# Memory attention and a gated convolution in one kernel: a new written order of all steps

## The chip, the cores and the metric

The kernel runs on one core of a Trainium2 chip. The core has TensorE (PE, with its weight loads PEld), VectorE (DVE), ScalarE (ACT), GpSimd (POOL) and SyncE (SP, which here only issues the DMAs). The metric is the device time in microseconds of one execution; less is better.

## What is computed

For each of 8 batches: attention over 32 memory slots per head (8 heads of 64 columns, 576 rows), then a gated convolution on the 512 joined columns.

```
a    = softmax(phi, axis=rows)                 # 576 x 32 per head
k_m, v_m = a.T @ k, a.T @ v                    # 32 x 64 per head
p    = softmax(q @ k_m.T / 8)                  # 576 x 32 per head
x    = p @ v_m, heads side by side             # 576 x 512
gate = sigmoid(sum over 5 taps of conv_w[k] * x shifted by k)
out  = (gate * (x @ w_val)) @ w_out
```

All inputs and the output are float32. conv_w, w_val and w_out are shared by all batches.

## The kernel before, in words

The body is a list of small functions, called steps (`@step`), and a string `ORDER` with 950 names. The last loop of the kernel walks through `ORDER` and calls each step with the numbers behind its name; `phi_max.0.1` is `phi_max(0, 1)`: batch 0, half 1. A star behind a name (`soft_sub.0.0*`) makes `pick(usual, other)` return the second engine that the step knows. Each engine works through its own instructions in the order in which the steps issued them, and waits by semaphores for what others make; so `ORDER` alone decides what stands in front of what on PE, DVE, ACT, POOL and in SP's one DMA queue. The order had been made by a planner outside the kernel; the planner is not part of it.

The steps of one batch b, in the order of the data (g is a half of the heads, s a half of the 576 rows, t and n a block of 128 columns, y a pair of blocks):

- `load_phi`, `load_kv`, `load_rest`, `load_q` issue DMAs. `phi_max` (DVE, L343) takes maxima, `phi_turn` (PE, L354) turns them, `phi_top` (DVE, L361) finishes, `phi_spread` (PE, L370) spreads them to all partitions, `phi_lay` (ACT) copies them, `phi_sub` (POOL, with a star DVE, L383) and `phi_exp` (ACT, L388) make the weights. For batch 0 these steps run by halves g.
- `slots` (PE, L397) multiplies the weights with k, v and a column of ones; `slots_inv` (DVE, L404 and L406) inverts the sums, `slots_scale` (DVE, or ACT with a star) scales, `slots_turn` (PE) and `slots_place` (ACT) turn the result into kvT.
- `scores` (PE, L447) multiplies q with it; `scores_turn` (DVE, L459) transposes 32x32 blocks into the tile st. Then the softmax over 32 slots: `soft_max` (DVE, L485), `soft_sub` (POOL, L492, DVE with a star), `soft_exp` (ACT, L497), `soft_sum` (DVE, L503), `soft_inv` (a small addition, L512 on DVE or L510 on ACT with a star, and the inverse L513), `soft_mul` (POOL, DVE with a star, L519), `soft_turn` (DVE, L525), which writes pT. For batch 0 they run by halves of the rows, so that `soft_turn.0.0` and `soft_turn.0.1` each give half of pT. `soft_high` (ACT) and `soft_low` (POOL, DVE with a star, L217) split pT into a rounded part pH and the rest pL.
- `val_rows` (PE, L547) multiplies v_m with w_val; `val_copy`, `val_high`, `val_low` bring it out of PSUM and split it (vwF, vwH, vwL).
- `value` (PE, L642, six matmuls) makes a block of x @ w_val. The gate of batch 0 is `taps` (products, L572), `conv` (PE, L585, 40 matmuls a half) and `sigmoid` (ACT, L632); those of the others are `mix` (PE, L598), five `tap` steps (ACT, then DVE L622; a star gives the last tap to ACT and POOL) and `open_gate` (ACT).
- `gated` (DVE L655, with a star ACT and POOL) multiplies value and gate, `gated_high` and `gated_low` split it (hH, hL), `project` (PE, L675, twelve matmuls) multiplies with w_out, `place` (ACT, with a star DVE) copies to SBUF, `store` issues the DMA out.

The shared weights come as float32 and are rounded in steps of their own: `load_w` (w is c, v or o for conv_w, w_val, w_out; block t), `narrow_size` (ACT, L273) and `narrow_round` (ACT, L286), `narrow_bits` (DVE, L278), `narrow_add` (POOL, L292), `narrow_done` (DVE, L301). conv_w then goes through `spread_taps` (PE, L308) and `place_taps` (ACT), w_out through `wo_high` (ACT) and `wo_low` (POOL, L217). `warm.n` (PE, L224) issues n matmuls whose result nobody reads.

PSUM holds four tiles b (one bank each) and two tiles cv (two banks each); conv and mix take both cv tiles, scores takes them as well, and a step that needs one waits until the last reader of it is done. Of raw weights four fit in SBUF, of k and v three halves.

```
    def pick(usual, other):
        return other if live["other"] else usual

    with tc.manual_schedule():
        for x in ORDER.split():
            name, *args = x.rstrip("*").split(".")
            live["other"] = x.endswith("*")
            steps[name](*(int(a) if a.isdigit() else a for a in args))
```

The functions as the program prints them:

Of the kernel before, what the change touches and what calls it, by code (L numbers as in the profile page):

```python
# [43 lines left out]
warm.8 phi_exp.0.0 narrow_round.v.2 place_taps.0 narrow_bits.v.2 narrow_add.v.2 narrow_done.v.2 slots.0.0
slots_inv.0.0 slots_scale.0.0* narrow_done.v.3 slots.0.1 slots_inv.0.1 load_w.v.1 narrow_size.v.1 spread_taps.1
load_q.0.0 narrow_round.v.1 place_taps.1 load_q.0.1 warm.2 slots_scale.0.1 slots_turn.0 slots_place.0 load_w.o.0
narrow_bits.v.1 narrow_add.v.1 scores.0 narrow_done.v.1 narrow_round.o.0 taps.0.0 scores_turn.0.0 load_w.o.2
narrow_size.o.0 soft_max.0.0 soft_sub.0.0* taps.0.1 narrow_bits.o.0 narrow_size.o.2 narrow_bits.o.2 turn_taps.0
lay_taps.0 load_kv.1.1 soft_exp.0.0 scores_turn.0.1 narrow_round.o.2 narrow_add.o.0 val_rows.0 phi_exp.1 load_rest.1
slots.1.1 soft_sum.0.0 soft_inv.0.0 soft_mul.0.0* val_copy.0.1 soft_turn.0.0 soft_max.0.1 soft_sub.0.1* val_copy.0.0  # L50
val_high.0.0 val_low.0.0* load_w.o.1 narrow_size.o.1 narrow_bits.o.1 soft_high.0.0 soft_low.0.0* soft_exp.0.1
load_w.o.3 narrow_add.o.2 val_high.0.1 val_low.0.1 narrow_round.o.3 narrow_size.o.3 soft_sum.0.1 soft_inv.0.1*
narrow_bits.o.3 conv.0.0 sigmoid.0.0.1 load_kv.1.0 soft_mul.0.1* soft_turn.0.1 slots.1.0 sigmoid.0.0.0 soft_high.0.1
slots_inv.1.1 slots_scale.1.1* slots_inv.1.0 slots_scale.1.0* narrow_add.o.3 narrow_done.o.3 load_phi.2 conv.0.1
slots_turn.1 phi_max.2 phi_turn.2 soft_low.0.1 value.0.0.1 phi_top.2 narrow_round.o.1 narrow_add.o.1 slots_place.1
sigmoid.0.1.1 sigmoid.0.1.0 phi_spread.2 narrow_done.o.2 phi_lay.2 phi_sub.2 narrow_done.o.1 wo_high.1 wo_low.1
load_q.1 scores.1.0 wo_high.2 gated.0.0.1 scores_turn.1.0 scores.1.1 scores_turn.1.1 val_rows.1 val_copy.1.0
val_copy.1.1 soft_max.1 soft_sub.1 load_phi.3 value.0.1.0 gated.0.1.0 phi_max.3 value.0.0.3 gated.0.0.3 value.0.0.2
gated.0.0.2 value.0.0.0 gated.0.0.0 narrow_done.o.0 value.0.1.1 phi_exp.2 phi_turn.3 phi_top.3 wo_low.2 soft_exp.1
soft_sum.1 val_high.1.0 load_rest.2 value.0.1.3 gated_high.0.0.0 gated_low.0.0.0 load_kv.2.1 slots.2.1 load_kv.2.0  # L60
slots.2.0 slots_inv.2.1 gated.0.1.1 wo_high.3 soft_inv.1* soft_mul.1* soft_turn.1 slots_scale.2.1* gated.0.1.3
gated_high.0.0.1 gated_low.0.0.1 slots_inv.2.0 slots_scale.2.0 phi_spread.3 phi_lay.3 wo_high.0 wo_low.0 wo_low.3
value.0.1.2 warm.2 soft_high.1 load_phi.4 gated.0.1.2 val_low.1.0 phi_max.4 mix.1.1 tap.1.1.1.0* tap.1.1.1.1
tap.1.1.1.2 tap.1.1.1.3 project.0.0.0 slots_turn.2 gated_high.0.1.0 place.0.0.0 gated_high.0.1.1 soft_low.1 load_q.2
gated_low.0.1.0 project.0.0.1 phi_turn.4 slots_place.2 val_rows.2 tap.1.1.0.0 tap.1.1.0.1 load_kv.3.1 tap.1.1.1.4
tap.1.1.0.2 val_high.1.1 val_low.1.1 place.0.0.1 val_copy.2.0 val_high.2.0 scores.2.0 open_gate.1.1.1 scores_turn.2.0
val_low.2.0 val_copy.2.1 project.0.0.3 place.0.0.3 tap.1.1.0.3 tap.1.1.0.4 gated_low.0.1.1 scores.2.1 project.0.0.2
place.0.0.2 scores_turn.2.1 mix.1.0 tap.1.0.0.0 phi_top.4 value.1.1.3 soft_max.2 gated.1.1.3 soft_sub.2 tap.1.0.0.1
tap.1.0.0.2 tap.1.0.1.0* tap.1.0.1.1 project.0.1.0 tap.1.0.1.2 tap.1.0.1.3 phi_sub.3 load_rest.3 tap.1.0.1.4
soft_exp.2 value.1.0.2 store.0.0.1 soft_sum.2 soft_inv.2 soft_mul.2 project.0.1.1 place.0.1.0 place.0.1.1 val_high.2.1  # L70
project.0.1.3 phi_spread.4 tap.1.0.0.3 tap.1.0.0.4 phi_lay.4 phi_exp.3 phi_sub.4 value.1.1.2 place.0.1.3 gated.1.1.2
soft_turn.2 project.0.1.2 open_gate.1.1.0 place.0.1.2 open_gate.1.0.1 slots.3.1 slots_inv.3.1 slots_scale.3.1
load_kv.3.0 slots.3.0 gated_high.1.1.1 slots_inv.3.0 gated_low.1.1.1 slots_scale.3.0 gated.1.0.2 open_gate.1.0.0
# [671 lines left out]
```

## Time and profile before

| what | us |
|---|---|
| median of 3 timed runs | 252.17 |
| lowest and highest of them | 251.85, 253.33 |
| the profiled execution, its own time | 251.45 |
| its span (first to last instruction) | 249.70 |

The profile shows one execution. Its span lies 1.75 us under its own time, which also holds the start and the end of the program. Lines as L343 are lines of the kernel; DVE is VectorE, ACT ScalarE, POOL GpSimd; times of rows are us from the start of the span unless marked ns. A matmul's end is modelled, so a busy PE need not be a PE at its peak; where the number of matmuls in a stretch counts, the start of the next one is used.

### The profile page before, as it was taken

How to read it: one execution, taken by the hardware profiler on the slowest of the kernel's cores; microseconds unless marked ns; L12 is line 12 of the kernel's file. 1: busy time of each engine (PE TensorE's matmuls, PEld its weight loads, DVE VectorE, ACT ScalarE, POOL GpSimd, SP SyncE). 2: the span in 40 equal slices, each digit the busy share in tenths (PEclk: the TensorE clock that was granted, in tenths of full speed). 3: DMA queues.
4: the chain of work that ended last, by engine and by line, in shares of the span. 5: the costliest groups of instructions: out<-in, count | busy, mean ns of one | idle time of the engine just before them, and what ended most of it. 6: DMA issues, size and time to landing. Idle time of an engine off the chain costs nothing.

```text
span 249.7 us, 6632 instructions
## 1 busy us (share of the span) xinstructions
PE 230.2 (92%) x2664; PEld 199.8 (80%) x2664; DVE 205.9 (82%) x413; ACT 182.5 (73%) x350; POOL 171.0 (68%) x128
## 2 busy tenths in 40 slices
...
GB/s 215 418 414 406 410 272 277 217 139 367 15 350 376 398 251 105 257 371 198 31 361 191 50 50 182 131 239 128 112 3 95 3 0 97 174 18 1 142 97 95
DMA packets 12142, 47.78 MB, mean 191 GB/s; under 512 B 1352, under 2 KB 1864, under 8 KB 9168
## 3 DMA queue, kind: packets, MB, share of 16 engines
...
## 4 chain that ended last, share of the span: by engine, by line
PE 73%; DVE 18%; ACT 2%; POOL 2%; issue 2%; DMA 1%; SPq 0%; POOLq 0%; DVEq 0%; ACTq 0%
PE b L675 39%; PE b L642 18%; PE cv L598 4%; PE b L397 3%; PE cv L447 3%; PE b L547 2%; DVE pT L525 2%; DVE st L519 2%; DVE gate L622 2%; DVE mx L343 1%; DVE ss L503 1%; DMA raw<-in_conv_w_dram 1%; PE cv L585 1%; DVE hH L301 1%; DVE st L459 1%
## 5 line engine op out<-in xcount | busy, mean ns | idle before, releaser
L622 DVE SCALAR_TENSOR_TENSOR gate<-cv,cwP,gate 128x288 f32<-128x288 f32 x200 | 87.4, 504 | 3.2 <-ACT gate L620 3.1
L675 PE MATMUL b<-hL,woH 128*128 128x288 f32 x256 | 76.4, 299 | 0.2 <-PE cv L598 0.2
L675 PE MATMUL b<-hH,woL 128*128 128x288 f32 x256 | 76.1, 297 | 0.0
L675 PE MATMUL b<-hH,woH 128*128 128x288 f32 x256 | 75.4, 294 | 0.0
L217 POOL TENSOR_TENSOR hL<-h,hH 128x576 fp32r<-128x576 f32 x31 | 44.8, 1455 | 12.1 <-ACT hH L214 7.0
L675 PEld LDWEIGHTS b<-hL,woH 128*128 128x128 f32 x256 | 48.1, 188 | 5.1 <-issue 2.0
L675 PEld LDWEIGHTS b<-hH,woL 128*128 128x128 f32 x256 | 48.1, 188 | 0.2 <-POOL woL L217 0.2
L675 PEld LDWEIGHTS b<-hH,woH 128*128 128x128 f32 x256 | 48.1, 188 | 0.0
L214 ACT COPY o<-b 128x288 f32<-128x288 f32 x50 | 19.6, 404 | 26.9 <-PE b L675 25.9
L642 PE MATMUL b<-pL,vwH 128*128 128x288 f32 x128 | 29.4, 311 | 0.0
L655 POOL TENSOR_TENSOR h<-h,gate 128x288 f32<-128x288 f32 x20 | 16.0, 809 | 17.6 <-ACT h L653 17.2
L642 PE MATMUL b<-pH,vwL 128*128 128x288 f32 x128 | 27.3, 295 | 0.0
L642 PE MATMUL b<-pH,vwH 128*128 128x288 f32 x128 | 27.3, 294 | 0.0
L655 DVE TENSOR_TENSOR h<-b,gate 128x288 f32<-128x288 f32 x44 | 18.9, 448 | 9.0 <-ACT gate L627 4.3
L620 ACT ACTIVATE gate<-cv,cwP 128x288 f32<-128x288 f32 x56 | 24.8, 506 | 0.4 <-PE cv L598 0.2
L642 PEld LDWEIGHTS b<-pL,vwH 128*128 128x128 f32 x128 | 20.1, 188 | 5.2 <-issue 1.7
L292 POOL TENSOR_TENSOR hH<-hH,hL 128x512 int32<-128x512 int32 (+1 forms) x9 | 12.8, 1424 | 16.4 <-DVE hH L278 9.0
L217 POOL TENSOR_TENSOR vwL<-vwF,vwH 128x512 fp32r<-128x512 f32 x14 | 18.4, 1313 | 8.1 <-ACT vwH L214 4.7
L627 ACT ACTIVATE gate<-gate 128x576 f32<-128x576 f32 x28 | 19.4, 696 | 5.4 <-DVE gate L622 4.5
L397 PE MATMUL b<-kv,e 128*32 128x129 f32 x512 | 19.0, 293 | 2.8 <-ACT e L388 2.7
L397 PEld LDWEIGHTS b<-kv,e 128*32 128x32 f32 x512 | 15.4, 141 | 7.2 <-ACT e L388 4.9
L642 PEld LDWEIGHTS b<-pH,vwL 128*128 128x128 f32 x128 | 20.5, 188 | 0.0
...
## 6 DMA issues: line engine op xcount, KB each, us to landing
...
```

What stands on the lines that cost most here:

```text
L214: eng.copy(out=out, in_=x) if eng is nc.scalar else eng.tensor_copy(out=out, in_=x)
L217: eng.tensor_tensor(out=out, in0=x, in1=hi.bitcast(F32), op=ALU.subtract)
L292: nc.gpsimd.tensor_tensor(out=a, in0=a, in1=r, op=ALU.add)
L397: nc.tensor.matmul(km[j * M:(j + 1) * M, 0:2 * D + 1], lhsT=e[:, g, j * M:(j + 1) * M, c], rhs=x[:, c, j, :] if c < C - 1 else rests[b % 2 ...
L447: nc.tensor.matmul(sc[t][j * M:(j + 1) * M, c, 0:HALF], lhsT=live["kvT", b][rows, x, j * M:(j + 1) * M], rhs=live["q", b][rows, x, j, :], ...
L598: nc.tensor.matmul(cv[g][x * D:(x + 1) * D, j // 2, 0:PAD + HALF], lhsT=live["kvd", b][rows, G, g], rhs=pTs[b % 2][rows, g, s * HALF:(s + ...
L620: nc.scalar.activation(out=o[:, t], in_=x, func=AF.Identity, scale=w)
L622: nc.vector.scalar_tensor_tensor(out=o[:, t], in0=x, scalar=w, in1=o[:, t], op0=ALU.mult, op1=ALU.add)
L627: nc.scalar.activation(out=gt, in_=gt, func=AF.Sigmoid)
L642: nc.tensor.matmul(vp[:, 0:HALF], lhsT=a[:, t // PG, n:n + P], rhs=p[:, g, s * HALF:(s + 1) * HALF], start=(i == 0), stop=(i == len(parts) ...
L655: eng.tensor_tensor(out=h[:, i], in0=x, in1=gt, op=ALU.mult)
L675: nc.tensor.matmul(ps[:, 0:HALF], lhsT=w[:, t, n * P:(n + 1) * P], rhs=a[:, t % 2], start=(i == 0), stop=(i == len(parts) - 1))
```

## The change

Only the string `ORDER` is new; it holds the same 950 steps. No function, tile or buffer count changes, and since the string has one line more, every line of the kernel below it has a number that is higher by 1. 45 steps lose their star and 47 others get one, so some steps change engine: `soft_sub.0.0` and `soft_sub.0.1` go from DVE to POOL, `taps.0.0` and `taps.0.1` from POOL to DVE, `soft_mul.6` from DVE to POOL, `val_copy` of batches 5 to 7 in one half each from ACT to DVE; 9 instead of 12 gates have the starred tap.

```diff
-load_phi.0.0 phi_max.0.0 phi_turn.0.0 load_phi.0.1 load_w.c.0 narrow_size.c.0 narrow_bits.c.0 phi_max.0.1 phi_turn.0.1
...
+load_phi.0.0 phi_max.0.0 phi_turn.0.0 phi_top.0.0 load_w.v.2 narrow_round.v.2 narrow_size.v.2 narrow_bits.v.2
+load_w.c.0 narrow_add.v.2 narrow_round.c.0 load_w.v.0 load_w.v.3 narrow_round.v.3 narrow_done.v.2 phi_spread.0.0
...
```

The DMA queue of SP, at the start of the program. First as it stood before (e is phi, raw a block of weights, kv and rest are k and v with their last rows):

```order
L234 DMA e<-in_phi_dram 128x640 x2
L259 DMA raw<-in_conv_w_dram 8x640
L234 DMA e<-in_phi_dram 128x1280
L259 DMA raw<-in_w_val_dram 128x1024 x3
L239 DMA kv_78<-in_kv_dram 128x2064
L244 DMA rest_81<-in_rest_dram 128x516
L239 DMA kv_79<-in_kv_dram 128x2064
L259 DMA raw<-in_w_val_dram 128x1024
L249 DMA q<-in_q_dram 128x1152 x2
```

and now:

```order
L235 DMA e<-in_phi_dram 128x640
L260 DMA raw<-in_w_val_dram 128x1024
L260 DMA raw<-in_conv_w_dram 8x640
L260 DMA raw<-in_w_val_dram 128x1024 x2
L235 DMA e<-in_phi_dram 128x640
L245 DMA rest_81<-in_rest_dram 128x516
L235 DMA e<-in_phi_dram 128x1280
L240 DMA kv_78<-in_kv_dram 128x2064
L240 DMA kv_79<-in_kv_dram 128x2064
L260 DMA raw<-in_w_val_dram 128x1024
L260 DMA raw<-in_w_out_dram 128x1024
L250 DMA q<-in_q_dram 128x1152 x2
L260 DMA raw<-in_w_out_dram 128x1024
```

Three blocks of w_val now stand behind the first half of phi and ahead of its second half, of all of batch 1's phi and of the first k and v; the fourth stays behind the second kv, and a block of w_out has moved ahead of q.

DVE, from the first transposition of batch 0's scores on (twelve rows each; st are scores, mm their maxima, ss their sums, pT the turned result). Before:

```order
L459 STREAM_TRANSPOSE st<-cv 128x2x288
L485 TENSOR_REDUCE mm<-st 128x18
L492 TENSOR_TENSOR st<-st,mm 128x2x288
L278 TENSOR_SCALAR hH<-hH 128x512 x2
L459 STREAM_TRANSPOSE st<-cv 128x2x288
L503 TENSOR_REDUCE ss<-st 128x18
L512 TENSOR_SCALAR ss<-ss 128x18
L513 RECIPROCAL ss<-ss 128x18
L519 TENSOR_TENSOR st<-st,ss 128x2x288
L525 STREAM_TRANSPOSE pT_74<-st 128x2x288
L485 TENSOR_REDUCE mm<-st 128x18
L492 TENSOR_TENSOR st<-st,mm 128x2x288
```

and now:

```order
L460 STREAM_TRANSPOSE st<-cv 128x2x288
L486 TENSOR_REDUCE mm<-st 128x18
L460 STREAM_TRANSPOSE st<-cv 128x2x288
L486 TENSOR_REDUCE mm<-st 128x18
L302 SCALAR_TENSOR_TENSOR hH<-raw,hH 128x512
L504 TENSOR_REDUCE ss<-st 128x18
L513 TENSOR_SCALAR ss<-ss 128x18
L514 RECIPROCAL ss<-ss 128x18
L279 TENSOR_SCALAR hH<-hH 128x512
L520 TENSOR_TENSOR st<-st,ss 128x2x288
L504 TENSOR_REDUCE ss<-st 128x18
L526 STREAM_TRANSPOSE pT_74<-st 128x2x288
```

Both halves are now transposed and searched for their maxima before either is summed; before, the second half's maximum stood behind the first half's way into pT (L525). The two subtractions L492 are no longer on DVE.

DVE around the softmax of batch 6, near 180 us. Before (o are finished blocks, hH rounded gated values):

```order
L503 TENSOR_REDUCE ss<-st 128x36
L214 COPY o<-b 128x288
L214 CAST hH<-h 128x576
L513 RECIPROCAL ss<-ss 128x36
L519 TENSOR_TENSOR st<-st,ss 128x1152
L525 STREAM_TRANSPOSE pT_74<-st 128x2x576
```

and now:

```order
L504 TENSOR_REDUCE ss<-st 128x36
L513 TENSOR_SCALAR ss<-ss 128x36
L514 RECIPROCAL ss<-ss 128x36
L623 SCALAR_TENSOR_TENSOR gate<-cv,cwP,gate 128x288 x4
L215 COPY o<-b 128x288
L623 SCALAR_TENSOR_TENSOR gate<-cv,cwP,gate 128x288 x2
L526 STREAM_TRANSPOSE pT_74<-st 128x2x576
```

The multiplication of st (L519) has left DVE, for POOL, and seven instructions, six for the taps and one for a block of output, stand between the inverse and the transposition.

## Rows read from the trace of the kernel before

**Rows 1.** The head of the page, the busy time of each engine over the span (with its share and number of instructions), and from the costliest groups VectorE's product of a value block with its gate (busy us and mean ns of one, then idle time before).

```profile
span 249.7 us, 6632 instructions
...
PE 230.2 (92%) x2664; PEld 199.8 (80%) x2664; DVE 205.9 (82%) x413; ACT 182.5 (73%) x350; POOL 171.0 (68%) x128
...
L655 DVE TENSOR_TENSOR h<-b,gate 128x288 f32<-128x288 f32 x44 | 18.9, 448 | 9.0 <-ACT gate L627 4.3
```

**Rows 2.** The busy time by stage. Columns: the stretch from and to in us, its length, then for each engine the busy us and the number of instructions, then the granted clock of TensorE as a share of full, the busy share of the DMA engines and GB/s.

```profile
0.00:24.19 24.19, 14.71 (x165) 10.53 (x165) 14.24 (x25) 11.34 (x21) 9.89 (x19) 1.00 0.93 362
24.19:37.65 13.46, 10.01 (x181) 6.65 (x180) 12.81 (x23) 10.60 (x18) 6.21 (x5) 0.62 0.83 341
37.65:56.14 18.49, 16.50 (x271) 13.28 (x271) 16.89 (x28) 14.16 (x27) 13.65 (x10) 1.00 0.60 212
56.14:178.79 122.65, 122.55 (x1419) 107.16 (x1420) 111.97 (x237) 107.75 (x209) 108.50 (x74) 1.00 0.56 210
178.79:184.18 5.39, 4.71 (x99) 4.29 (x97) 5.31 (x6) 2.39 (x4) 2.25 (x2) 1.00 0.15 58
184.18:246.13 61.95, 61.76 (x535) 57.85 (x535) 44.73 (x98) 35.88 (x72) 30.46 (x22) 1.00 0.18 67
246.13:249.70 3.57, 0.00 (x0) 0.00 (x0) 0.00 (x0) 0.40 (x1) 0.00 (x0) 1.00 0.29 98
```

**Rows 3.** The chain of work that ended last, in order of time: start us, us, what (engine, tile, line).

```profile
54.76 1.39 DVE pT L525
...
56.20 0.75 PE cv L598 x16
...
180.24 2.48 DVE st L519
...
184.18 0.83 PE cv L598 x16
...
246.13 0.40 ACT o L214
```

**Rows 4.** Instructions in order of time, all engines, 0 to 26 us: start us, us, engine, line, operation, out<-in, count, and in brackets the idle time before it and what ended it.

```profile
3.61 0.82 DVE L343 TENSOR_REDUCE mx<-e 128x128 f32<-128x640 f32 x1 [3.61 <-DMA e<-in_phi_dram]
...
4.70 0.48 ACT L273 ACTIVATE hH<-raw 8x320 f32<-8x320 f32 x1 [2.67 <-DMA raw<-in_conv_w_dram]
...
8.32 0.66 ACT L286 ACTIVATE hL<-raw 128x512 int32<-128x512 uint32 x1 [2.76 <-DMA raw<-in_w_val_dram]
...
10.85 1.43 PE L308 MATMUL b<-taps,kvT 8*128 8x320 f32 x2
...
11.16 0.41 DVE L278 TENSOR_SCALAR hH<-hH 128x512 int32<-128x512 int32 x1
...
11.72 1.27 POOL L292 TENSOR_TENSOR hH<-hH,hL 128x512 int32<-128x512 int32 x1 [4.59 <-DVE hH L278]
...
13.02 0.69 DVE L301 SCALAR_TENSOR_TENSOR w_val_sb<-raw,hH 128x512 int32<-128x512 int32 x1 [1.12 <-POOL hH L292]
...
15.65 1.51 DVE L278 TENSOR_SCALAR hH<-hH 128x512 int32<-128x512 int32 x1
...
16.25 1.76 PE L397 MATMUL b<-kv,e 128*32 128x129 f32 x32
...
22.84 2.15 POOL L572 TENSOR_TENSOR taps<-cwB,kvd 128x320 f32<-128x320 f32 x2
...
22.94 1.33 DVE L301 SCALAR_TENSOR_TENSOR w_val_sb<-raw,hH 128x512 int32<-128x512 int32 x1 [1.50 <-POOL hH L292]
...
24.19 0.77 DVE L459 STREAM_TRANSPOSE st<-cv 128x576 f32<-128x576 f32 x1
```

**Rows 5.** The same view from 25 to 38 us, VectorE and, in the second row, ScalarE.

```profile
25.00 0.75 DVE L485 TENSOR_REDUCE mm<-st 128x18 f32<-128x576 f32 x1
...
26.57 0.68 ACT L497 ACTIVATE st<-st 128x576 f32<-128x576 f32 x1 [1.63 <-DVE st L492]
...
27.83 0.70 DVE L503 TENSOR_REDUCE ss<-st 128x18 f32<-128x576 f32 x1
...
28.57 1.07 DVE L512 TENSOR_SCALAR ss<-ss 128x18 f32<-128x18 f32 x1
...
29.98 0.76 DVE L519 TENSOR_TENSOR st<-st,ss 128x576 f32<-128x576 f32 x1
...
30.77 0.78 DVE L525 STREAM_TRANSPOSE pT<-st 128x576 f32<-128x576 f32 x1
...
36.87 0.78 DVE L525 STREAM_TRANSPOSE pT<-st 128x576 f32<-128x576 f32 x1
```

**Rows 6.** The same view for rows of GpSimd, ScalarE and VectorE between 26 and 54 us, and as the last row VectorE's maximum over a whole batch's scores between 56 and 246 us from the groups by line and form (busy us and mean ns of one, idle before).

```profile
26.96 2.65 POOL L292 TENSOR_TENSOR hH<-hH,hL 128x512 int32<-128x512 int32 x2 [1.96 <-DVE hH L278]
...
35.61 1.28 ACT L632 ACT_TABLE_LOAD   x1
...
46.90 2.15 POOL L492 TENSOR_TENSOR st<-st,mm 128x1152 f32<-128x1152 f32 x1
...
49.04 1.80 DVE L301 SCALAR_TENSOR_TENSOR hH<-raw,hH 128x512 int32<-128x512 int32 x1
...
53.37 1.36 DVE L519 TENSOR_TENSOR st<-st,ss 128x1152 f32<-128x1152 f32 x1
...
L485 DVE TENSOR_REDUCE mm<-st 128x36 f32<-128x1152 f32 x6 | 8.1, 1345 | 0.1
```

More of the change, by code (lines that the diff above doesn't have):

```diff
@@ L44 @@
[L44 to L73, printed above, removed]
@@ new lines @@
+tap.1.1.1.4 phi_max.4 soft_high.1 scores.2.0 scores_turn.2.0 place.0.0.1 scores_turn.2.1 project.0.1.0 phi_exp.3
+phi_turn.4 load_kv.3.0 place.0.1.1* phi_top.4 soft_max.2 place.0.1.0 mix.1.0 tap.1.0.0.0* load_kv.3.1 store.0.1.0
+slots.3.0 slots_inv.3.0 tap.1.0.0.1 soft_low.1 slots_scale.3.0* tap.1.0.0.2 val_rows.2 val_copy.2.1 tap.1.0.0.3
+slots.3.1 val_copy.2.0 slots_inv.3.1 soft_sub.2 load_q.3 value.1.1.0 gated.1.1.0 soft_exp.2 soft_sum.2 tap.1.0.1.0
+tap.1.0.1.1 project.0.1.3 slots_scale.3.1* place.0.1.3 value.1.1.1 tap.1.0.0.4 gated.1.1.1* soft_inv.2* tap.1.0.1.2
@@ new lines @@
+phi_spread.4 soft_mul.2 tap.1.0.1.3 project.0.1.2 load_phi.5 phi_max.5 val_high.2.1 project.0.0.3 load_rest.4
+slots_turn.3 open_gate.1.0.0 phi_lay.4 phi_sub.4 place.0.1.2 place.0.0.3 value.1.0.0 store.0.0.1 slots_place.3
+gated_high.1.1.0 tap.1.0.1.4 soft_turn.2 val_high.2.0 open_gate.1.1.1 value.1.1.3 gated_low.1.1.0 gated.1.1.3*
+scores.3.0 scores_turn.3.0 open_gate.1.0.1 gated.1.0.0* scores.3.1 scores_turn.3.1 soft_high.2 value.1.1.2 gated.1.1.2
+value.1.0.2 mix.2.1 gated.1.0.2* value.1.0.1 gated_high.1.1.1 gated_low.1.1.1 load_kv.4.0 tap.2.1.0.0 tap.2.1.1.0
@@ new lines @@
+tap.2.0.0.2 project.1.1.1 tap.2.0.1.0* tap.2.0.1.1 tap.2.0.1.2 tap.2.0.1.3 soft_low.2 load_kv.5.1 val_low.3.1
+project.1.0.1 place.1.0.1 open_gate.2.1.1 tap.2.0.0.3 tap.2.0.0.4 project.1.1.0 slots_scale.4.1* place.1.1.0
+place.1.1.1 project.1.0.0 place.1.0.0 soft_mul.3 soft_turn.3 phi_spread.5 tap.2.0.1.4 open_gate.2.1.0 value.2.1.3
+phi_lay.5 slots_turn.4 slots_place.4 val_high.3.0 value.2.1.1 value.2.1.2 gated.2.1.2 soft_high.3 gated.2.1.1
+value.2.1.0 store.1.1.0 gated.2.1.0 mix.3.1 tap.3.1.0.0 phi_sub.5 gated_high.2.1.0* gated_low.2.1.0 val_low.3.0
@@ new lines @@
+store.3.0.0 slots.7.1 slots_inv.7.1 gated.5.0.1 slots.7.0 gated_low.5.1.0 slots_inv.7.0 soft_high.6* soft_low.6
+place.4.1.3 store.4.1.1 mix.6.1 tap.6.1.0.0 slots_scale.7.1 slots_scale.7.0* value.5.0.0 gated.5.0.0 value.5.0.3
+gated.5.0.3* tap.6.1.0.1 tap.6.1.0.2 tap.6.1.0.3 tap.6.1.1.0* project.4.1.1 place.4.1.1* tap.6.1.0.4 project.4.1.0
+place.4.1.0 gated_high.5.0.0 value.6.1.0 tap.6.1.1.1 gated_high.5.0.1* gated_low.5.0.1 slots_turn.7 project.5.1.3
+gated_low.5.0.0 tap.6.1.1.2 slots_place.7 scores.7.0 tap.6.1.1.3 tap.6.1.1.4 store.4.1.0 val_rows.7 open_gate.6.1.0
```

162 lines of the change are left out of this document (86 added, 76 removed).

## The prediction

> **What bounds the kernel now.** I read the page's first lines, then the busy time by stage, then the chain that ended last, then the instructions in order of time up to 56 us. The page shows TensorE busy for 92% of the span and VectorE for 82% [rows 1]; such averages hide where the time is lost, so the stages come next. From 56.14 to 178.79 PE is busy for 122.55 of 122.65 us, and from 184.18 to 246.13 for 61.76 of 61.95 [rows 2]. In these two stretches no order of steps can help: PE has the same matmuls in both versions. What is left to win lies in the first 56 us, in the 5.39 us between the two stretches (PE 4.71), and in the 3.57 us of the last eviction and store, which stay, since both orders end with the same project, place and store.
>
> In the first 56 us DVE is the engine to watch. Up to 24.19 it waits much (14.24 busy), from 24.19 to 37.65 it works 12.81 of 13.46, from 37.65 to 56.14 it works 16.89 of 18.49 [rows 2]. The chain says the same: it runs through DVE until the transposition of batch 1's softmax (54.76 + 1.39), and at 56.20 the first mix of batch 1 starts on PE, from where PE is full; the only later place where it leaves PE for long is 180.24 to 184.18, DVE's multiplication and transposition for batch 6 [rows 3]. All matmul steps that stand ahead of mix.1.1 in the old order stand ahead of it in the new one too. So the question is: when does mix.1.1 start, and does PE stay full afterwards?
>
> **Leg 1, to the first transposition of scores (24.19 [rows 4]).** The new order loads block 2 of w_val right behind the first half of phi and puts the second half of phi behind three w_val blocks. Block 2 is now second in line; I take 5.5 us for its landing, between conv_w's first use (4.70, third in line before) and block 3's (8.32, fifth) [rows 4]. Then two conversions on ACT of 0.66, bits 0.41, POOL's add 1.27, done 0.69 [rows 4]: 9.2. Behind it on DVE come phi_sub (0.8), bits (0.41), the maximum of the second half (0.8), its turn and top (0.9), bits of conv_w (0.3), the maximum of batch 1 (twice 0.8): 14.2. PE then spreads the taps twice at 1.4 us a pair and phi once, ACT lays and copies (0.4 each) and exponentiates (0.7): the first slots start near 18.0 instead of 16.25 [rows 4], and the two of them end near 21.2. Inverse, scaling, turn, copy and scores add 3.5 us, and DVE has the two taps products (now its own, 0.5 each by DVE's 0.448 for 288 columns [rows 1], 1.07 each if as slow as on POOL [rows 4]), two done and one bits in the same time: 25.2 for the transposition, 1.0 late. Bounds: 0.5 early if block 2 lands at 4.7 and done no longer waits for POOL's taps product (below), 2.5 late if it lands at 8.3. In the row 24.19 to 37.65 the granted clock is 0.62 of full [rows 2]; so TensorE ran at both of its levels, 1.2 and 2.4 GHz, there. The change moves the eight warming matmuls from ahead of the first slots to just ahead of the first conv, so the first slots may run at 1.2 GHz; the stretch from 18.0 to 21.2 holds that for most of it.
>
> **Leg 2, the first batch's softmax (24.19 to 37.65, 13.46 us).** Before, the second half's maximum stands behind the first half's transposition into pT. Now both halves are turned and searched first, and the subtractions go to POOL. DVE's list between the two points is: two transpositions of 0.77, two maxima of 0.75, a done 0.69, two sums of 0.70, a small addition and an inverse (0.45), two bits (0.8), two multiplications (1.5), a transposition 0.78, a second inverse with a wait for ACT's addition (0.6), a second done 0.69, slots' inverse 0.3, the transposition 0.78 [rows 5]. Together 11.0. POOL's subtraction of a half (half of the 2.15 us row of 128x1152, so 1.07 [rows 6]; between 0.8 and 1.4) and ACT's exponential (0.68) lie under the second transposition, second maximum and done (2.2). I add 0.7 for one meeting with POOL: 11.7, 1.75 less than before. The second half's pT is ready at 36.9, 0.75 early. PE gets little of that itself, since conv.0.1 also waits for the sigmoids behind a table load (1.28 at 35.61 [rows 6]); DVE gets it.
>
> **Leg 3, to batch 1's softmax (37.65 to 56.14, 18.49 us).** The new list on DVE is: two low parts 1.4, bits 0.4, inverse 0.3, four scalings 1.1, a maximum of phi 1.47, two done 1.3, top 0.4, gated 0.45, two transpositions 1.44, maximum 1.35, two gated 0.9, phi's next maximum 1.47, three gated 1.2, top 0.4, sum 1.35, a low part 0.76, inverse 0.37, multiplication 1.36, transposition 1.38: 18.85, of one length with the old stretch although that one waited 1.6 us. The scalings, two low parts and the first halves' work have moved into it. Add one half of a meeting with POOL, 0.65: 19.5. So batch 1's transposition ends at 36.9 + 19.5 = 56.4 instead of 56.14: **0.3 us late**. The ends: 24.19 - 0.5 + 11.0 + 18.85 = 53.5 with no meeting at all, and 24.19 + 2.5 + 12.1 + 20.5 = 59.3 with a meeting of 1.1 in leg 2 and one and a half in leg 3.
>
> **POOL beside DVE.** The done step at 22.94 takes 1.33 us where the same at 13.02 takes 0.69; POOL has started a product at 22.84. The bits step at 15.65 takes 1.51 against 0.41, the addition on 18 columns at 28.57 1.07 beside POOL's add from 26.96 [rows 4 to 6]. At 49.04 a done takes 1.80, and at 180.24 the multiplication takes 2.47, 1.1 over the 1.36 of 53.37 [rows 3, 6]. Each time DVE ends shortly after POOL. The Trainium skill ("SBUF — State Buffer", Who interferes with whom) says that a DVE instruction with two SBUF inputs, or in a two-port mode, and a GpSimd instruction lock each other out for a whole instruction, and that the first one wins; the rows agree, and by that rule moving subtractions to POOL would speak against the change wherever DVE multiplies or finishes weights beside them. My sum counts two meetings, 0.7 and 0.65.
>
> **Leg 4, the rest.** Batch 6's multiplication stands on DVE before, behind a place that waits for PE and beside POOL (2.47). Now it is POOL's (2.15) with DVE free for taps, and some 17 us of matmuls (six project, six value, two slots and a mix step) stand between its scores and its mix. The 5.39 us stretch cost PE 0.7 and the slower issue around it 0.5 [rows 2]: 1.2 gained, or nothing if POOL's own queue is late. Against it I set 0.3 for new short waits at the places where scores need the PSUM tiles of the taps: by the same sums, DVE and PE meet there within half a microsecond in both orders. Sum: +0.3 - 1.2 + 0.3 = **-0.6 us**. The profiled execution took 251.45 us (span 249.7), so a like one takes 250.85; the median of the three timed runs is 252.17, 0.7 above it, and against that I forecast 251.6.
>
> **Rivals.** *The early start works fully.* Every leg at its lower end: 53.5, 2.6 early; with 0.9 from leg 4, 3.5 us less: 248.7. For it: the DMA engines are busy for 0.93 and 0.83 of the first two stretches [rows 2] and the new order asks for no byte more, so no load is late but the second half of phi; against it: five meetings with POOL in the rows of before, which no order of so full engines avoids entirely.
> *POOL takes the place of the wait.* Between the subtraction for batch 1 and mix.1.1 POOL now has the four low parts of w_out and one of the values in a row, with no gap, and beside them DVE does a done, a low part and the multiplication, each with two SBUF inputs. Three further meetings at 1.1 (the price of 49.04 and 180.24) give +3.3: 254.9, slower. From one further meeting on the new kernel is slower than the old, from three on by over 1%. For it: exactly these operations met before; against it: in the row at 53.37 DVE came first and lost nothing [rows 6].
> *Nothing arrives.* Leg 2's gain is eaten by leg 1 and the sigmoids, and batch 6 finds another late operand: 252.2.
> *The full stretches break.* VectorE and TensorE are both nearly full from 56 to 150; a new order could make PE wait half a microsecond at each of some seven mixes: +3 and 255. For it: the order of each batch changed; against it: by the durations of before, DVE's work ahead of the last transposition of batches 3 to 7 is the same to within 1 us in both lists (for batch 2 there are 2 us more, behind 4 us more of matmuls).
>
> **How the numbers follow.** A measurement of this kernel tells about 1%, 2.5 us, from no change. Forecast 0.50 (250 to 253.3, all within 1%), full early start 0.19, POOL 0.13, nothing 0.12, broken stretches 0.06. The early start lies just beyond -1% in most of its range; the POOL case mostly beyond +1%, the broken stretches too. So faster 0.19, same 0.64, slower 0.17. The range reaches into the first two rivals: 249.3 to 254.2.
>
> **What would show it.** In the new profile: first transposition of scores at 25.2 (24 to 26.5), second half's pT at 36.9, mix.1.1 at 56.4, no PE gap near 180, subtractions of 1.07 on POOL. A mix.1.1 before 54.5 or after 58.3 makes the sum wrong; a PE that is not full between 60 and 180 makes leg 4 wrong; a DVE row of 1.7 or 2.4 beside POOL ahead of mix.1.1 is the second rival.

## The result and the profile after

| | before | after |
|---|---|---|
| median of 15 timed runs (us) | 251.77 | 255.12 |
| lowest and highest | 251.32, 253.33 | 253.43, 257.64 |
| after over before, 95% interval | | 1.013 (1.010 to 1.015) |
| the profiled execution | 251.45, span 249.70 | 257.64, span 255.5 |

The new order is 1.3% slower. The forecast was 251.6, within 1%, in a range up to 254.2. The profiled execution of the new order is the slowest of its fifteen, 2.5 us above their median, so a second profile of the same order (new_again, 256.24) stands beside it below. Ratios are taken over undisturbed runs, medians over all. Lines of the new order are those of the old plus 1.

The head of the page of the new order, which answers to [rows 1]:

```profile
span 255.5 us, 6625 instructions
PE 230.9 (90%) x2664; PEld 199.1 (78%) x2664; DVE 212.1 (83%) x420; ACT 179.2 (70%) x342; POOL 175.5 (69%) x129
```

TensorE's busy time grew by 0.7 us on the same 2664 matmuls, VectorE's by 6.2 us on 7 more instructions. Part of such growth is waiting inside instructions, which the page counts as busy; the stages tell where. The busy time by stage, cut at the same events as [rows 2] (first transposition of scores, second half's pT, mix.1.1, then the stretches of TensorE); columns as there:

```profile
0.00:26.32 26.32, 13.04 (x139) 7.73 (x139) 15.42 (x28) 11.45 (x21) 10.16 (x19) 1.00 0.90 338
26.32:36.92 10.60, 8.61 (x188) 6.59 (x188) 10.00 (x21) 9.22 (x16) 6.98 (x5) 1.00 1.00 385
36.92:58.29 21.37, 17.68 (x300) 12.98 (x292) 20.64 (x30) 14.72 (x25) 16.47 (x12) 1.00 0.64 236
58.29:106.95 48.66, 48.66 (x577) 42.01 (x577) 45.66 (x90) 43.75 (x88) 38.88 (x26) 0.96 0.65 236
106.95:109.26 2.31, 0.00 (x1) 0.00 (x1) 2.31 (x5) 0.02 (x1) 2.31 (x2) 1.00 0.96 398
109.26:178.79 69.53, 69.53 (x791) 60.79 (x792) 62.17 (x132) 55.95 (x111) 57.04 (x40) 0.98 0.45 159
178.79:184.18 5.39, 5.39 (x43) 5.39 (x42) 5.06 (x12) 5.35 (x8) 4.82 (x3) 1.00 0.29 83
...
59.49:62.90 3.41, 3.41 (x17) 3.41 (x16) 3.41 (x9) 3.10 (x9) 0.01 (x1) 0.50 0.97 370
110.69:114.10 3.41, 3.41 (x20) 2.89 (x13) 3.33 (x9) 2.62 (x7) 3.19 (x3) 0.50 0.70 286
```

The first three rows are the prediction's legs 1, 2 and 3, the last up to mix.1.1. Leg 1 took 26.32 us for 24.19, leg 2 10.60 for 13.46, leg 3 21.37 for 18.55 (37.65 to 56.20). The stretch at 178.79 to 184.18, where PE was busy for 4.71 of 5.39, is full. New are a wait of PE of 2.31 us ahead of 109.26, and two stretches with a granted clock of 0.50 (1.2 GHz), one behind each of the two long waits.

The chain of the new order, in order of time (start us, us, what), answering to [rows 3]:

```profile
58.29 0.75 PE cv L599 x16
59.04 6.50 PE b L676 x36
...
88.89 3.17 PE b L676 x24
...
97.56 3.74 DVE ss L513
...
109.26 0.75 PE cv L599 x16
...
111.28 4.66 PE b L676 x24
```

24 project matmuls take 3.17 us at full clock, so 36 take 4.76. Behind mix.1.1 they took 6.50, 1.74 more; behind 109.26 24 took 4.66, 1.49 more. That makes the account. The start of mix.1.1 is 2.09 us late (+2.13 - 2.86 + 2.82); 1.74 and 1.49 went to the lower clock; 2.31 to the new wait: 7.63. The last matmul ends 6.17 late (252.30 for 246.13), so the rest of the plan gained 1.46. Leg 4 is in that, but how much of it is leg 4's isn't measured in this order; in the old order its place alone gave 0.5 (fix6, below).

In new_again mix.1.1 starts at 58.16, the wait ahead of the third batch's mix is 2.34 us (109.39), the granted clock is 0.50 in one stretch only (59.89 to 63.30), and the last matmul ends at 250.90. Late start and wait thus came in both profiles of the order; the second low stretch came in one execution and not in the other.

The places on VectorE, all engines in order of time (start us, us, engine, line, operation, out<-in), answering to [rows 4 to 6]. A meeting is a VectorE instruction that takes longer beside a GpSimd instruction than alone; a done step is `narrow_done`, the last of a weight's rounding:

```profile
14.26 1.16 DVE L302 SCALAR_TENSOR_TENSOR taps<-raw,hH 8x320 int32<-8x320 int32 x1
...
18.11 2.46 POOL L384 TENSOR_TENSOR e<-e,mxa 128x1280 f32<-128x1280 f32 x1
18.19 2.93 DVE L302 SCALAR_TENSOR_TENSOR w_val_sb<-raw,hH 128x512 int32<-128x512 int32 x1 [1.37 <-POOL hH L293]
...
18.87 1.96 PE L398 MATMUL b<-kv,e 128*32 128x129 f32 x32
...
41.71 2.50 DVE L302 SCALAR_TENSOR_TENSOR hH<-raw,hH 128x512 int32<-128x512 int32 x2 [0.48 <-POOL hH L293]
...
50.03 5.58 POOL L218 TENSOR_TENSOR woL<-hH,woH 128x512 fp32r<-128x512 f32 x4
...
52.57 1.87 DVE L218 TENSOR_TENSOR hL<-h,hH 128x576 fp32r<-128x576 f32 x1
...
54.76 2.06 DVE L520 TENSOR_TENSOR st<-st,ss 128x1152 f32<-128x1152 f32 x1
...
97.34 2.66 POOL L218 TENSOR_TENSOR pL<-pT,pH 128x1152 fp32r<-128x1152 f32 x1
...
97.56 3.73 DVE L513 TENSOR_SCALAR ss<-ss 128x36 f32<-128x36 f32 x1
...
99.97 1.28 POOL L218 TENSOR_TENSOR vwL<-vwF,vwH 128x512 fp32r<-128x512 f32 x1
```

Read VectorE's row against GpSimd's above or below it. The addition on 36 columns starts 0.22 us after GpSimd's low part of 2.66 us, and ends at 101.29, 0.04 after GpSimd's second instruction. In the old order the same addition for the same batch took 0.16 with GpSimd idle:

```profile
97.71 0.16 DVE L512 TENSOR_SCALAR ss<-ss 128x36 f32<-128x36 f32 x1
```

In leg 3 two done steps take 2.50 for 1.38, a low part 1.87 for 0.76, the multiplication 2.06 for 1.36: 2.9 us in three meetings.

### The profile page after: what moved, and what is told of

The parts are those of the page before. It is cut to its first block, busy times and chain, and to the rows that moved or that the text cites. A ratio compares the mean times of both kernels' runs of the same rounds, so it can differ in the third digit from the quotient of the medians.

```text
span 255.5 us, 6625 instructions
## 1 busy us (share of the span) xinstructions
PE 230.9 (90%) x2664; PEld 199.1 (78%) x2664; DVE 212.1 (83%) x420; ACT 179.2 (70%) x342; POOL 175.5 (69%) x129
## 4 chain that ended last, share of the span: by engine, by line
PE 62%; DVE 14%; POOL 7%; DMA 5%; issue 5%; ACT 4%; SPq 1%; POOLq 0%; DVEq 0%; ACTq 0%
PE b L676 34%; PE b L643 14%; PE b L398 5%; PE cv L599 3%; DVE gate L623 3%; DMA raw<-in_w_val_dram 3%; PE cv L448 3%; DMA raw<-in_w_out_dram 3%; PE b L548 2%; POOL hH L293 1%; DVE ss L513 1%; DVE pT L526 1%; DVE hH L302 1%; DVE w_val_sb L302 1%; POOL hL L218 1%
## 5 line engine op out<-in xcount | busy, mean ns | idle before, releaser
L623 DVE SCALAR_TENSOR_TENSOR gate<-cv,cwP,gate 128x288 f32<-128x288 f32 x206 | 90.1, 507 | 1.8 <-ACT part L621 1.0
L676 PE MATMUL b<-hL,woH 128*128 128x288 f32 x256 | 77.8, 304 | 0.0
L676 PEld LDWEIGHTS b<-hL,woH 128*128 128x128 f32 x256 | 49.2, 192 | 2.9 <-DVE h L656 1.1
L676 PEld LDWEIGHTS b<-hH,woH 128*128 128x128 f32 x256 | 49.4, 193 | 0.0
L676 PEld LDWEIGHTS b<-hH,woL 128*128 128x128 f32 x256 | 49.4, 193 | 0.0
L218 POOL TENSOR_TENSOR hL<-h,hH 128x576 fp32r<-128x576 f32 x29 | 41.2, 1430 | 11.3 <-ACT hH L215 6.7
L293 POOL TENSOR_TENSOR hH<-hH,hL 128x512 int32<-128x512 int32 (+1 forms) x9 | 11.6, 1303 | 18.4 <-DVE hH L279 13.9
L218 POOL TENSOR_TENSOR vwL<-vwF,vwH 128x512 fp32r<-128x512 f32 x15 | 20.3, 1358 | 2.4 <-ACT vwH L215 2.4
L218 POOL TENSOR_TENSOR pL<-pT,pH 128x1152 fp32r<-128x1152 f32 (+1 forms) x8 | 20.2, 2526 | 2.2 <-DVE pH L215 2.2
L643 PEld LDWEIGHTS b<-pH,vwH 128*128 128x128 f32 x128 | 20.5, 187 | 0.0
```

The lines of the kernel that those rows point to most:

```text
L218: eng.tensor_tensor(out=out, in0=x, in1=hi.bitcast(F32), op=ALU.subtract)
L293: nc.gpsimd.tensor_tensor(out=a, in0=a, in1=r, op=ALU.add)
L623: nc.vector.scalar_tensor_tensor(out=o[:, t], in0=x, scalar=w, in1=o[:, t], op0=ALU.mult, op1=ALU.add)
L643: nc.tensor.matmul(vp[:, 0:HALF], lhsT=a[:, t // PG, n:n + P], rhs=p[:, g, s * HALF:(s + 1) * HALF], start=(i == 0), stop=(i == len(parts) ...
L676: nc.tensor.matmul(ps[:, 0:HALF], lhsT=w[:, t, n * P:(n + 1) * P], rhs=a[:, t % 2], start=(i == 0), stop=(i == len(parts) - 1))
```

## The experiments

Theory M: VectorE waits beside GpSimd set the late mix.1.1 and the wait at 109. Rivals: the loads or the first leg alone; fixed waits of the new plan of another cause. All kernels but no_pl2 change the order alone. Where two orders are joined, steps that the first part has issued are left out of the second.

**The new order again, and halves of it.** new_again is the unchanged new order. start_new and rest_new join the two orders at mix.1.1:

```diff
 # start_new
-for x in OLD:
+for x in NEW up to mix.1.1, then OLD without the steps already issued:
 # rest_new
+for x in OLD up to mix.1.1, then NEW without the steps already issued:
```

> The new order once more, unchanged, beside the three others. Theory M (meetings of VectorE with GpSimd decide): the time is again about 255.1 with a spread of some 4 us between executions, and in this profile the late start (mix.1.1 at 57 to 58.5) is seen again, while the stall of 2.3 us near 109 comes only if the small addition of batch 3's softmax meets GpSimd again. Rival P (the new plan has fixed waits of its own): 255.1 too, but with both, the late start and the stall near 109, at the same places and of the same size.

> The new order up to mix.1.1, then all remaining steps in the old order. The first profile of the new order has mix.1.1 2.1 us late and 1.7 us more from matmuls at a lower granted clock behind the wait there. If the start is the whole cause: 255.1. If the start costs what that profile shows: 251.8 + 2.1 to 3.8 = 253.9 to 255.6, with the old stall near 180 to 184 still there. If the rest of the plan is the cause (rival P): 251.8 to 252.5.

> The old order up to mix.1.1, then all remaining steps in the new order. Mix.1.1 should start at 56.2 as before. Theory M: 251.8 less 1.2 (the stall near 180 is gone) = 250.6, plus up to 3.8 (2.3 of stall near 109 and 1.5 of lower clock behind it) in executions in which the addition for batch 3 is held up: 250.6 to 254.4, with a wide spread. Start as the whole cause: 250.6 and a narrow spread. Rival P: 254 to 255, narrow.

Measured beside 251.56 for the old order: new_again 256.05 (ratio 1.015, 1.012 to 1.018), start_new 254.67 (1.011, 1.008 to 1.015), rest_new 254.09 (1.009, 1.006 to 1.012). In new_again the addition took 3.76 us again: in both profiles of the unchanged order the meeting comes back at the same place and size, as rival P has it. start_new shows mix.1.1 at 57.51 and the old wait at 186, and the start alone loses 3.1 us. rest_new has mix.1.1 at 56.29, but two waits of PE (1.21 at 63.89, 1.28 at 92.70) that neither order has, so this run doesn't say what the new rest is worth. It does show that the wait at 109 isn't in the order behind mix.1.1 by itself. There the addition has the same two GpSimd instructions beside it, but starts 1.63 us into the first for 0.22:

```profile
95.63 2.66 POOL L218 TENSOR_TENSOR pL<-pT,pH 128x1152 fp32r<-128x1152 f32 x1
...
97.26 1.07 DVE L513 TENSOR_SCALAR ss<-ss 128x36 f32<-128x36 f32 x1
98.24 1.29 POOL L218 TENSOR_TENSOR vwL<-vwF,vwH 128x512 fp32r<-128x512 f32 x1
```

It takes 1.07, comes through between the two, and PE has no wait ahead of that mix. So the order decides which instructions meet, and the price differed with the moment at which they met.

**The wait at 109.** inv3_act moves the addition to ScalarE; no_pl2 leaves VectorE as it was and takes away GpSimd's instruction (batch 2's low part isn't computed).

```diff
 # inv3_act
-soft_inv.3
+soft_inv.3*
 # no_pl2, in soft_low
+if b == 2:
+    live["pL", 2] = live["pL", 1]
+    return
```

> The new order with one star more: the small addition on 128x36 ahead of batch 3's inverse is done on ScalarE instead of VectorE, where it took 3.73 us in the profile (0.16 before). Theory M: the stall of 2.3 near 109 and the 1.5 of lower clock behind it go: 255.1 - 3.8 = 251.3 if every execution had them, 253.2 if half had. Rival P (another instruction is late there, or ScalarE's queue holds the addition up as long): 254.6 to 255.1.

> The new order with one instruction of GpSimd left out: the low part of batch 2's probabilities is not computed (batch 1's stands in its place). Nothing that VectorE does is changed. Theory M (the small addition at 97.6 is held up by GpSimd's low part of 2.66 us and the 1.28 us one behind it): the addition meets only the second one, 0.2 to 1.3 us for 3.73, mix.3.1 at 106.5 to 107.2 for 109.3, stall near 109 under 0.5 us; time 255.1 to 256.0 less 1.9 to 2.3 = 252.8 to 254.1. Rival (the addition waits for its operand or its own engine): 3.7 us again, stall of 2.3 again, 255 to 256.

inv3_act: 253.92 (1.009, 1.006 to 1.012), above the 251.3 to 253.2 that I gave. I had taken 1.9 to 3.8 from 255.1; new_again, which ran beside it, took 256.05, and from there the gain is 2.1. no_pl2: 253.02 (1.004, 1.001 to 1.007) beside 251.69, inside what theory M gave. First inv3_act, then no_pl2, the rows around the addition and the mix behind it (in no_pl2 lines from L536 on are higher by 3):

```profile
96.19 2.66 POOL L218 TENSOR_TENSOR pL<-pT,pH 128x1152 fp32r<-128x1152 f32 x1
96.44 0.32 ACT L511 ACTIVATE ss<-ss,eps 128x36 f32<-128x36 f32 x1 [1.21 <-DVE ss L504]
...
106.44 0.75 PE L599 MATMUL cv<-pT,kvd 32*64 32x292 f32 x16
```

```profile
95.33 1.29 POOL L218 TENSOR_TENSOR vwL<-vwF,vwH 128x512 fp32r<-128x512 f32 x1
95.55 1.10 DVE L513 TENSOR_SCALAR ss<-ss 128x36 f32<-128x36 f32 x1
...
104.81 0.75 PE L602 MATMUL cv<-pT,kvd 32*64 32x292 f32 x16
```

On ScalarE the addition takes 0.32 beside the same 2.66 us instruction. On VectorE it takes 1.10 with one GpSimd instruction beside it, for 3.73; in both kernels PE has no wait ahead of the mix. (The profile of no_pl2 is of its fastest execution, 251.55.) That GpSimd makes this wait is shown from both sides.

**Leg 3.** quiet3 is inv3_act with the low part of pT's second half on VectorE, and the first gated low part behind batch 1's transposition.

```diff
-soft_low.0.1
+soft_low.0.1*
-gated_low.0.0.0* ... soft_inv.1* soft_mul.1* soft_turn.1
+soft_inv.1* soft_mul.1* soft_turn.1 gated_low.0.0.0*
```

> The new order with the star on batch 3's small addition, and with three of leg 3's meetings changed: batch 0's low part of the first gated block (1.87 us on VectorE beside GpSimd at 52.6) stands behind batch 1's transposition instead of ahead of its inverse, and the low part of pT's second half goes from GpSimd, where it stands beside the two done steps at 41.7 (2.50 us for 1.37), to VectorE. If VectorE's work with its meetings sets mix.1.1: 1.1 less at 41.7, 0.75 more for the low part, 1.87 less ahead of the inverse, that is 2.2 earlier, at most: mix.1.1 at 56.0 to 57.3 for 58.2, time 253.9 - 1.0 to 2.2 = 251.7 to 252.9. If something else sets it (the weights from GpSimd, the values on ScalarE): no change, 253.5 to 254.

253.00 (1.007, 1.004 to 1.010) beside 251.65. In its profile the three places, and then the first project:

```profile
41.71 1.29 DVE L302 SCALAR_TENSOR_TENSOR hH<-raw,hH 128x512 int32<-128x512 int32 x2 [0.52 <-POOL hH L293]
...
53.01 1.49 DVE L520 TENSOR_TENSOR st<-st,ss 128x1152 f32<-128x1152 f32 x1
...
55.83 1.68 DVE L218 TENSOR_TENSOR hL<-h,hH 128x576 fp32r<-128x576 f32 x1
...
58.19 0.40 PE L676 MATMUL b<-hL,woH 128*128 128x288 f32 x1 [1.48 <-DVE h L656]
```

The done steps take 1.29 for 2.50 and the multiplication 1.49 for 2.06; leg 3 is 19.04 us and mix.1.1 starts at 55.96 for 58.47 in inv3_act. So VectorE with its meetings did set mix.1.1. But the low part meets GpSimd at its new place, and the project waits 1.48 us behind it: of 2.5 us, 0.9 came out in the median against inv3_act, and 253.00 is just above the range given. GpSimd now pays at the multiplication:

```profile
49.49 6.17 POOL L218 TENSOR_TENSOR woL<-hH,woH 128x512 fp32r<-128x512 f32 x4
```

The four low parts of w_out took 5.58 us in the new order. Here the fourth takes 2.44 for 1.29: it starts beside the multiplication, and the multiplication comes first.

**Legs alone.** leg1_new and leg23_new cut the two orders at the first transposition of scores. leg1_b and leg23_b do the same with the blocks of w_val and w_out renamed, so that both orders finish them in one sequence. The two orders have the eight warming matmuls on different sides of the cut: leg1_new and leg1_b issue them not at all, leg23_new, leg23_b and combo (below) twice.

```diff
 # leg1_new, leg1_b
+for x in NEW up to scores_turn.0.0, then OLD without the steps already issued:
 # leg23_new, leg23_b
+for x in OLD up to scores_turn.0.0, then NEW up to mix.1.1, then OLD, each without the steps already issued:
```

> The new order up to the first transposition of scores (the w_val loads ahead of the first k and v are in it), then the old order. Theory L (the loads and what stands around them are late, and the lateness is carried on): the transposition comes at 25.7 to 26.3 instead of 24.2, mix.1.1 at 57.7 to 58.3, the time 251.6 + 1.5 to 2.1 = 253.1 to 253.7, and 1.7 more in executions with a stretch of lower clock behind the wait. Theory H (the late start comes from leg 3 of the new order, the first leg's lateness is taken up by waits of the old legs, which were 1.6 us in leg 3): mix.1.1 at 56.2 to 56.8, the time 251.6 to 252.2.

> The old order up to the first transposition of scores, then the new one (the two halves of batch 0's softmax free of each other) up to mix.1.1, then the old one. In the first trace of the new order leg 2 took 10.6 us for 13.46 and leg 3 21.3 for 18.49. Theory L (legs 2 and 3 together are no later than the old ones): transposition at 24.2, second half's pT at 34.8 to 35.5, mix.1.1 at 55 to 56.2, time 250.4 to 251.6. Theory H (the meetings with GpSimd in leg 3 are the cause): mix.1.1 at 57.5 or later, time 253 or more.

> Leg 1 of the new order with everything behind it in the old order, now with the blocks of the weights renamed so that both orders finish them in the same sequence (leg1_new waited 17.6 us in leg 2 for blocks that the two orders load in a different sequence). Theory L (the new loads make leg 1 late by 2 us and the old legs 2 and 3 can't take it up): transposition at 25.7 to 26.3, mix.1.1 at 58 to 58.3, time 251.65 + 1.9 = 253.5. Rival (the old legs have waits to take it up): mix.1.1 at 56.2 to 57, 251.7 to 252.4.

> The same for legs 2 and 3: old order up to the first transposition of scores (at 24.2 then), new order with renamed blocks up to mix.1.1, old order behind it. By the two traces of the new order leg 2 is worth -2.9 and leg 3 costs +2.8: mix.1.1 at 56.1, time 251.6 (250.9 to 252.3). If leg 3's meetings with GpSimd do not come at the shifted times: leg 3 shorter by up to 2.9, mix.1.1 at 53.2, 249 to 250. If the halves free of each other gain nothing with the old loads (leg 2 13 us): 254.

leg1_new took 257.94 (1.024, 1.020 to 1.028): its second half's pT is ready only at 43.66, since the old leg 2 waited for blocks that the new leg loads later. leg23_new took 254.68 (1.010, 1.007 to 1.013), with the transposition at 27.18 behind a rounding whose block had not landed. Both tell of the join, not of the legs. Renamed, beside 251.69: leg1_b 253.68 (1.007, 1.005 to 1.010), leg23_b 255.10 (1.013, 1.010 to 1.016). First the three legs of leg1_b, then legs 2 and 3 of leg23_b:

```profile
0.00:26.77 26.77, 13.23 (x139) 7.92 (x139) 15.40 (x27) 11.44 (x22) 10.15 (x19) 1.00 0.90 338
26.77:39.84 13.07, 9.55 (x176) 5.97 (x176) 12.42 (x22) 10.56 (x18) 5.23 (x4) 0.74 0.84 329
39.84:58.65 18.81, 16.83 (x299) 13.13 (x292) 17.12 (x29) 14.19 (x28) 14.26 (x10) 1.00 0.56 210
```

```profile
24.23:36.27 12.04, 8.26 (x138) 6.35 (x144) 11.59 (x23) 9.46 (x17) 7.00 (x5) 0.89 0.97 389
36.27:58.88 22.61, 19.18 (x347) 14.79 (x331) 20.66 (x31) 14.71 (x25) 15.79 (x12) 0.99 0.56 206
```

leg1_b: the lateness of leg 1 passes through the old legs whole (13.07 + 18.81 = 31.88 for 13.46 + 18.55 = 32.01 before), as theory L has it. leg23_b: the new legs lose 2.6 us behind the old leg 1 (34.65 for 32.01), with the meetings of leg 3 unchanged (2.50, 1.82, 2.05 us). None of its three cases expected that much; it is on the side of leg23_new's theory H. Leg 2 gains 1.4 us there (12.04 for 13.46), not the 2.9 of the new order, so behind the old leg 1 only half of that gain is seen. The parts' losses, 2.0 and 3.4 us, add up to more than that of the start as a whole (3.1 in start_new), so they are not terms of one sum: in leg23_b VectorE also waits 1.13 us for slots behind conv matmuls that ran at a granted clock of 0.50.

**Why leg 1 is late.** conv_early is quiet3 with conv_w's rounding moved up.

```diff
-narrow_round.c.0 ... phi_turn.0.1 narrow_size.c.0 ... narrow_bits.c.0 narrow_add.c.0 ... phi_max.1 narrow_done.c.0 ... spread_taps.1 ... place_taps.1
+narrow_round.c.0 narrow_size.c.0 narrow_bits.c.0 narrow_add.c.0 ... phi_sub.0.0* narrow_done.c.0 spread_taps.1 ... place_taps.1
```

> quiet3 with conv_w's rounding (size, bits, addition, done) and its first spreading on TensorE moved up, directly behind the first block of w_val, as it stood early in the old order (done at 10.03 there, at 14.26 in the new order). Theory T: leg 1 is late because this chain is: the done step ends at 15.4, TensorE's spreading for the taps stands ahead of the spreading of batch 1's maximum and of the first slots, and these wait for the copies by ScalarE (slots at 18.87 for 16.25). Then the done step comes at 9 to 10.5, the slots at 16.3 to 17.5, the transposition of scores at 24.5 to 25.5, and the time is 253.0 less 0.8 to 2: 251.0 to 252.2. Rival (k and v land later because three blocks of w_val are loaded ahead of them): slots at 18 or later, 252.7 to 253.3.

252.62 (1.002, 1.000 to 1.005): the marks came as theory T has them, the time 0.4 above its range. In the profile:

```profile
9.89 0.48 DVE L302 SCALAR_TENSOR_TENSOR taps<-raw,hH 8x320 int32<-8x320 int32 x1
...
17.34 1.96 PE L398 MATMUL b<-kv,e 128*32 128x129 f32 x32
...
24.92 0.78 DVE L460 STREAM_TRANSPOSE st<-cv 128x576 f32<-128x576 f32 x1
...
56.64 0.40 PE L676 MATMUL b<-hL,woH 128*128 128x288 f32 x1 [1.48 <-DVE h L656]
```

The done step of conv_w comes at 9.89 for 14.26, and with it the slots 1.5 and the transposition 1.4 us earlier than in the new order, with the loads as they were. The six profiles with the new leg 1 unchanged (after, new_again, start_new, inv3_act, no_pl2, quiet3) have the transposition at 25.70 to 26.63, all later than 24.92. 0.7 us of leg 1's 2.1 are left; the slots start 1.1 later than before and are not explained further. mix.1.1 starts at 54.41, 1.8 us earlier than in the old order, and the project again waits 1.48.

**Versions that should win.** fix6 is the old order with leg 4's place alone; combo joins the old leg 1, legs 2 and 3 as in quiet3, and fix6's rest; conv_low moves conv_early's low part to GpSimd.

```diff
 # fix6
-soft_sum.6 project.4.0.1 place.4.0.1* gated_high.5.1.0* soft_inv.6* soft_mul.6* value.5.0.2 soft_turn.6
+soft_sum.6 soft_inv.6* soft_mul.6* project.4.0.1 place.4.0.1* soft_turn.6 gated_high.5.1.0* value.5.0.2
 # conv_low
-gated_low.0.0.0*
+gated_low.0.0.0        # between wo_low.1 and wo_low.3
```

> The old order with one place changed: batch 6's inverse and multiplication stand ahead of the block of output and the cast that wait for TensorE, the transposition behind that block. Leg 4 alone, then. If the 5.39 us stretch at 179 to 184 is worth the 1.2 us that I put on it: 250.4. If the moved instructions only shift the wait to the block of output and the project behind it: 251.6.

> What the runs so far leave as gains, put together: old leg 1, new legs 2 and 3 with the two low parts moved as in quiet3 (mix.1.1 came 2.5 us earlier there, and the first project waited 1.5 for the low part), and behind mix.1.1 the old order with the edit of fix6 (-0.5). If all of it adds up: mix.1.1 at 53.6 to 54.0, first project 0.9 earlier than before, time 251.65 - 0.9 - 0.5 = 250.2. If the project's low part or the weights of w_out from GpSimd set the end instead: 251 to 251.7.

> conv_early with batch 0's low part of the first gated block on GpSimd, between the first and the second block of w_out, instead of on VectorE behind batch 1's transposition (there it took 1.69 us beside GpSimd, held up the product of values and gate behind it, and the first project waited 1.48 us for that product). If that is what the project waits for: project at 55.0 to 55.6 for 56.64, no stretch of lower clock behind it, time 252.6 less 1.1 to 1.9 = 250.7 to 251.5, below the old order's 251.7. If GpSimd's four blocks of w_out, now 1.4 us later, set the project's start: 56 to 56.6 and 252 to 252.6.

fix6: 251.17 beside 251.65, ratio 0.998 (0.996 to 1.000), the only kernel below the old order, by 0.5 us for the 1.2 expected; its interval just reaches no change. combo: 253.81 (1.009, 1.006 to 1.012); its mix.1.1 comes at 56.6, far from 53.6 to 54. conv_low: 253.18 (1.006, 1.004 to 1.009). First fix6, then conv_low:

```profile
182.25 1.11 PE L397 MATMUL b<-kv,e 128*32 128x129 f32 x32 [0.49 <-ACT o L214]
```

```profile
55.33 1.12 PE L398 MATMUL b<-kv,e 128*32 128x129 f32 x32 [1.80 <-ACT mxa L215]
...
57.01 3.04 DVE L218 TENSOR_TENSOR hL<-h,hH 128x576 fp32r<-128x576 f32 x1
57.27 0.40 PE L676 MATMUL b<-hL,woH 128*128 128x288 f32 x1
...
60.10 0.40 PE L676 MATMUL b<-hL,woH 128*128 128x288 f32 x1 [1.77 <-DVE hL L218]
```

In fix6 a shorter wait (0.49 for 0.68) stands ahead of the slots instead of the mix. In conv_low the first project does start right behind mix.1.1 (57.27), so the 1.48 is gone. Two other waits stand in its place. With one more instruction on GpSimd the low parts of w_out come later; ScalarE waits 2.19 us for one of them, and PE 1.80 for ScalarE's copy behind that, so mix.1.1 itself starts at 56.60 for 54.41. Then the next low part in VectorE's list meets two GpSimd instructions, 3.04 us for 0.76, and the project stops half way for 1.77, until 60.10. So the cured place hands its wait on.

Taken together: the meetings make the wait at 109 (shown from both sides) and most of leg 3's loss (shown by moving them); conv_w's late rounding makes two thirds of leg 1's. With all three places changed (conv_early) the new order is 0.9 us above the old one, for 4.5 in new_again. Open are the rest of leg 1, what a new leg 1 and new legs 2 and 3 share of their losses, the worth of the new rest by itself, and which of the two engines comes first when VectorE waits between two GpSimd instructions.

## Why the prediction was wrong, point by point

- **Leg 1, forecast 25.2, came 26.32.** Block 2 landed at 5.1 (5.5 forecast) and phi_sub ended at 9.6. The step that failed is "the first slots start near 18.0": I had conv_w's bits in VectorE's list but not its done step, which started at 14.26 and took 1.16 beside GpSimd. The taps' spreading on PE waited for it (15.56), and the slots began at 18.87. conv_early shows that this chain is two thirds of the lateness. The two slots then took 3.9 us for 3.2; their matmuls took 422 ns at the median for 274, though the granted clock stands at 1.00 in that stretch of both profiles. (The list up to conv_w's bits and batch 1's maximum adds up to 14.0, not to the 14.2 given.)
- **Leg 2, forecast 11.7, came 10.60.** The mechanism held: the halves are free of each other, and no VectorE instruction of leg 2 took longer beside GpSimd, so the 0.7 for a meeting was not needed. That the pT of the second half is ready at 36.92, as forecast (36.9), is luck: leg 1 was 1.1 too short in the sum and leg 2 1.1 too long.
- **Leg 3, forecast 19.5, came 21.3 to the end of the transposition.** The term that was mis-sized is "one half of a meeting with POOL, 0.65": three meetings cost 2.9. That was the second rival in its mechanism, with "a done, a low part and the multiplication" and a price of 1.1 each, and it had 0.13. That its 254.9 lies so near the measured 255.12 is in part luck: it has mix.1.1 some 3.6 us late, which came 2.09 late, and neither the wait at 109 nor the clock. The argument against it, that the multiplication came first once in the old order, was one case. But the four blocks of w_out in a row don't settle it either: quiet3 has the same row, and there the multiplication comes first.
- **Leg 4.** The wait at 180 to 184 went as forecast: the stretch is full. The 1.2 put on it isn't shown; fix6 gave 0.5. "0.3 for new short waits" failed: the addition for batch 3 took 3.73 and PE waited 2.31. The two lists were compared "by the durations of before", and in that comparison the addition is 0.16. A list of durations is blind to which neighbour stands beside an instruction, and that is what a new order changes. It is the broken-stretches rival (0.06), at one mix only.
- **The clock** was no term of the sum behind leg 1; it was put at nothing without a reason. A late operand of 1.75 or 2.31 us cost PE 1.74 or 1.49 more behind it in the profile shown.
- **The total.** In the profiled execution +2.09 for the start (+0.3 forecast), +2.31 for the wait and 3.2 for the clock (0.3 for all new waits), -1.46 for the rest (-1.2). The clock also sorts the executions. One low stretch of 3.41 us at 0.50 takes 0.007 off the mean granted clock of the span. Of the fifteen executions on record two have a mean of 1.000 (253.44 and 253.69), eleven 0.993 (median 255.12) and two 0.987 (257.34 and 257.64): by that the median holds one low stretch, the profiled execution two. The eleven spread from 253.43 to 257.21, so the clock isn't all. Of the signs named in the prediction, two came: PE isn't full between 60 and 180, and VectorE has slow rows beside GpSimd ahead of mix.1.1 (1.87, 2.06, 2.50). The third just did not: mix.1.1 at 58.29 lies under the 58.3 given.
